# A fused attention and two-layer feed-forward kernel: the first stage issued in an order written out by hand

## The chip, the cores and the metric

The kernel runs on one core of one Trainium2 chip, as one launch. The metric is the time of the launch on the device in microseconds (us), lower being better: the median of three runs.

## What is computed

Attention with a narrow window plus pooled blocks, then a maxout layer, then a mish layer. All inputs and outputs are float32 except the six weight matrices, which are float64 and are handed over as pairs of 32-bit words. Shapes: q, k, v are 4 x 8 x 768 x 64; the tokens are 3072 with 512 features; the hidden widths are 768 and 2048.

```python
def _attn_ref(q, k, v):
    block, window = (32, 16)
    k_sum = k.reshape(B, H, nb, block, D).max(axis=3)
    v_sum = v.reshape(B, H, nb, block, D).mean(axis=3)
    scores_l = scale * np.matmul(q, k.transpose(0, 1, 3, 2))
    mask_l = np.abs(pos[:, None] - pos[None, :]) < window
    scores_s = scale * np.einsum('bhsd,bhnd->bhsn', q, k_sum) + np.log(block)
    scores_all = np.concatenate([np.where(mask_l, scores_l, -1e9), scores_s], axis=-1)
    a = softmax(scores_all)
    return np.matmul(a, np.concatenate([v, v_sum], axis=2))

def _moe_ref(x, w1, w2, w3, w_out):
    h = np.maximum(np.maximum(x @ w1, x @ w2), x @ w3)
    return h @ w_out

def _moe2_ref(x, w_in, w_out):
    h = x @ w_in
    return (h * np.tanh(softplus(h))) @ w_out
```

## The kernel before

**Tiles and blocks.** The 3072 tokens are 48 tiles of 64; two tiles make a unit `u` (24 units, six to a batch), and three units, 384 tokens, make one of eight blocks. A unit goes through attention in five steps (`step`, L528): scores and exps of the next unit (`s2`, L435), preparation of q and k (`q_prep`, `k_prep`), transposes of the probabilities (`s3`, L490; the tile is `ptp`, its copy `pT`), normalisation (`s2b`, L480), and the product with v (`s4`, L501; `xp`, split into `xh` and `xl`). A block goes through `gemm1` (L587; products `hp`, three for each of six row groups f, combined by maxima into `m`, split into `hh` and `hl`) and `gemm2` (L624; product `yp`, one for each of four column groups e, over all six f, written to DRAM as `x2d`). At the end a second layer runs over all tokens (`g3`, `mish_a` to `mish_c`, `g4`).

**Precision.** Each product is made of three matmuls on a high and a low part of each operand. The high and low parts of x and h come from a cast on ScalarE and a difference on VectorE.

**Weights.** Each slice of a float64 weight matrix (128 x 512 values, 512 KB) is a job with four parts: a fetch into one of three `words` buffers (`fetch`, L163, SyncE), the magnitude on ScalarE (`size_of`, L174, writes `wa`), five or six VectorE operations that turn the words into a float32 value and a rest (`narrow`, L180), and the split into high and low part (`done`, L229). For the first 14 jobs the low part is made by three matmuls (`wp`, L240 to L242) and a ScalarE cast (L243); for the others by a difference on VectorE (L237). The 24 jobs of the first layer fill slots `a`, `b` (w1 to w3, three jobs for each f) and `c` (w_out, one for each f); 32 more, for the second layer, follow from block 2 on and go to DRAM. `run_job` (L203) moves each job in flight on by one part.

**Keys and values of batch 0.** They are loaded whole (L763, L768). The first six tiles take their keys from these copies through GpSimd (`load_k`, L401). Later tiles read them from a transposed copy in DRAM: `store_far` (L370) writes it (`kTd`), `load_k` reads it back (L404). The block means of v are six pairs of matmuls into `vp` (L306), copied by L788 and L790. Batches 1 to 3 are prepared while the batch before runs; KLOAD0 and VLOAD0 (L525, L526) say at which unit of batch 0.

**What sets the order.** The program is written in one order (L761 on), and a scheduler that models the engines reorders the instructions of each engine before the kernel is built. On the chip each engine then executes its list in order and waits on semaphores. All DMAs are issued by SyncE, in its list's order; each issue also waits until an earlier DMA on the same one of eight semaphores has landed. The written order before: loads, six `k_prep`, unit 0 up to `s2b`, three jobs in between, the six means of v, then 16 attention steps with a job at every second one (`PER`, L802 to L806), then block after block: a job, a group of the products, and as many attention steps as are due (L846 to L852).

**Buffers.** PSUM has four banks for `hp`, `yp` and `wp` together (tag `g`) and four for attention. `m` and `y` share two buffers. `words` has three.

Of the kernel before, what the change touches and what calls it, by code (L numbers as in the profile page):

```python
# [3 lines left out]

# [6 lines left out]
F32 = mybir.dt.float32  # L11
# [8 lines left out]
P = 128  # L20
# [11 lines left out]
NEAR = 6  # L32
BT = 6
ITEMS = 5
PER = [1, 0]
AHEAD = 4
JOBN = 3
JOB0 = 2
# [15 lines left out]
def tile_kernel(ctx, tc, q, k, v, w1, w2, w3, w_out, w_in2, w_out2, out):  # L54
# [87 lines left out]

    last = {"early": True}

# [53 lines left out]
        nc.vector.tensor_tensor(out=a, in0=w, in1=a, op=ALU.add)  # L198
        return a, None

    fetched, sized, narrowed = [], [], []

    def run_job(after=None):  # L203

        if narrowed:
            w, rest, done = narrowed.pop(0)
            done(w, rest)
        if jobs:
            src, done, parts = jobs.pop(0)
            fetched.append((fetch(src), done, parts))  # L210
        if sized:
            words, a, done, parts = sized.pop(0)
            narrowed.append((*narrow(words, a, parts), done))
        if fetched and (len(fetched) > 1 or not jobs):
            words, done, parts = fetched.pop(0)
            with tc.issue_after(after) if after else nullcontext():
                a = size_of(words)
            sized.append((words, a, done, parts))

    def busy():  # L220
        return bool(jobs or fetched or sized or narrowed)

    jobs = []
    fslice = lambda f: slice(f * P, (f + 1) * P)
# [3 lines left out]
    def into(tag, place, key):  # L228
        def done(w, rest):  # L229
            if tag not in slot_of:  # L230
                slot_of[tag] = wslot(tag)
            t = slot_of[tag]
            wa[key] = t, 2 * place
            h, l = t[:, 2 * place], t[:, 2 * place + 1]
            nc.scalar.copy(h, w)
            if rest is None:
                nc.vector.tensor_tensor(out=l, in0=w, in1=h.bitcast(F32), op=ALU.subtract)  # L237
                return
            sums = gps.tile([P, 512], F32, name="wp", tag="g")
            nc.tensor.matmul(sums, lhsT=ident, rhs=w, start=True, stop=False)  # L240
            nc.tensor.matmul(sums, lhsT=one_r, rhs=rest, start=False, stop=False)
# [17 lines left out]
    def keep(f, i):  # L259
        def done(w, _):  # L260
            h = stage.tile([P, 512], F32R, name="wr", tag="wr", bufs=AB)
            nc.scalar.copy(h, w)
            nc.vector.tensor_tensor(out=w, in0=w, in1=h.bitcast(F32), op=ALU.subtract)
            nc.sync.dma_start(out=w2d[f][:, 2 * i], in_=h.bitcast(F32))
            last["store"] = nc.sync.dma_start(out=w2d[f][:, 2 * i + 1], in_=w)

        return done

# [163 lines left out]
    att_t = {}  # L432
    heads = lambda s: s.rearrange("q (r p) x -> q r p x", r=2)

    def s2(u):  # L435

        t = u % NG
        kind = "first" if t == 0 else "last" if t == NG - 1 else "mid"
        mask = masks[kind]
        sc = [bank("sc") for r in range(2)]  # L440
        add = u >= PEMASK
        if not add:
            for r in range(2):
                for j, m in enumerate(split_masks[kind]):
                    nc.tensor.matmul(
                        sc[r][:, :, 0:KX], lhsT=one_r, rhs=m.unsqueeze(1).to_broadcast([P, NP, KX]),
                        start=(j == 0), stop=False,
                    )
        for p in range(NP):
            for e in reversed(range(GT)):  # L450
                for r in range(2):
                    d = slice(r * D, (r + 1) * D)
                    c = slice(e * QT, (e + 1) * QT)
                    nc.tensor.matmul(
                        sc[r][c, p, 0:KX], lhsT=qT[u % RQ][d, p, c], rhs=kT[(GT * u + e) % RK][d, p],
                        start=add, stop=add or p == NP - 1,
                    )
        s = ap2.tile([P, H, KX], F32, name="s", tag="s", bufs=SB)
        src = [x[:, :, 0:KX] for x in sc]
        if add:  # L460
            for r in range(2):
                wide = mask.unsqueeze(1).to_broadcast([P, NP, KX])
                nc.vector.tensor_tensor(out=heads(s)[:, r], in0=src[r], in1=wide, op=ALU.add)
            src = [heads(s)[:, r] for r in range(2)]
        nm = ap2.tile([P, 2, NP], F32, name="nm", tag="nm")
        if add:
            nc.vector.tensor_reduce(out=nm, in_=heads(s), axis=AX.X, op=ALU.max, negate=True)  # L467
        else:
            for r in range(2):
                nc.vector.tensor_reduce(out=nm[:, r], in_=src[r], axis=AX.X, op=ALU.max, negate=True)  # L470
        sm = ap2.tile([P, H], F32, name="esum", tag="esum")
        for h in range(H):
            r, p = divmod(h, NP)
            nc.scalar.activation(  # L474
                out=s[:, h], in_=src[r][:, p], func=AF.Exp, bias=nm[:, r, p : p + 1], accum_out=sm[:, h : h + 1]
            )
        rs = ap2.tile([P, H, 1], F32, name="rs", tag="rs")
        att_t[u] = (s, sm, rs)

    def s2b(u):  # L480
        s, sm, rs = att_t.pop(u)
# [40 lines left out]

    KLOAD = {0: [0, 1], 1: [2, 3], 2: [4, 5]}
    VLOAD = {0: [0], 1: [1], 2: [2], 3: [3, 4, 5], 4: [6, 7]}
    KLOAD0 = {1: [0, 1], 2: [2, 3], 3: [4, 5]}  # L525
    VLOAD0 = {1: [0], 2: [1], 3: [2], 4: [3, 4, 5]}  # L526

    def step(u):  # L528

# [2 lines left out]
        more = b + 1 < B  # L532

        def first():
            if u == 1:
                store_far()
            for T in (GT * (u + 1), GT * (u + 1) + 1):
                if ok(u + 1):
                    load_v(T)
            if ok(u + 1):  # L540
                s2(u + 1)

        def second():
            if ok(u + 2):
                q_prep(*divmod(u + 2, NG))
            for g in more and kload.get(t - 1) or ():
                k_prep(b + 1, g)
            if ok(u + 3):
                load_nat("q", q, *divmod(u + 3, NG))
            for g in more and kload.get(t) or ():  # L550
                load_nat("k", k, b + 1, g)

# [6 lines left out]
        def fourth():  # L559
            for g in more and vload.get(t - 1) or ():  # L560
                if b:
                    make_vsum(b + 1, *VP[g])
                else:
                    v_prep(1, g)
            for g in more and vload.get(t) or ():
                if b:
                    load_vsum(b + 1, *VP[g])
                else:
                    load_nat("v", v, 1, g)
            s3(u, 1)  # L570

        def fifth():
            s4(u)
            for T in (GT * (u + 2), GT * (u + 2) + 1):
# [49 lines left out]
    def gemm2(i, e):  # L624
# [13 lines left out]
            nc.sync.dma_start(out=x2d[i][:, e, :], in_=y[:, :n])  # L638

        return [emit]  # L640


    N2 = 384
# [117 lines left out]
    for g in range(NG):  # L761
        nat["k", 0, g] = t = room[g].rearrange("p (h d) -> p h d", h=H)
        nc.sync.dma_start(out=t, in_=k[0, :, g * P : (g + 1) * P, :].rearrange("h p d -> p h d"))  # L763
        if g == 2:
            load_nat("q", q, 0, 0)
    run_job()
    for g in range(NG):
        nc.sync.dma_start(out=vroom[g], in_=v[0, :, g * P : (g + 1) * P, :].rearrange("h p d -> p h d"))  # L768
        if g == 2:
            run_job()  # L770
    load_nat("q", q, 0, 1)
    for g in range(NG):
        k_prep(0, g, kst[g])
    for T in range(RK):
        load_k(T)
    q_prep(0, 0)
    run_job()
    s2(0)
    load_v(0)
    load_v(1)  # L780
    s2b(0)
    q_prep(0, 1)
    run_job()
    load_nat("q", q, 0, 2)
    vp = aps.tile([P, H, D], F32, name="vp", tag="a")
    for g in range(NG):
        mean_v(vp[0:NB].rearrange("p h d -> p (h d)"), vroom[g], g * NS, NB, g == 0, g == NG - 1)
    nc.scalar.copy(vr[0][0:NB], vp[0:NB])  # L788
    for t in vr[1:]:
        nc.gpsimd.tensor_copy(t[0:NB], vr[0][0:NB])  # L790

    steps = [it for u in range(NU) for it in step(u)]
    nstep = nit = 0

    def attend(upto):
        nonlocal nstep
        while nstep < min(upto, len(steps)):
            steps[nstep]()
            nstep += 1

    IB = ITEMS * BT // GT
    while nstep < IB + 1:  # L802
        attend(nstep + 1)
        for _ in range(PER[nit % len(PER)]):
            run_job()
        nit += 1  # L806

    later = [(f, (lambda f=f: wslot(slots[f])) if f < 2 * NF1 else (lambda f=f: extra[f - 2 * NF1]))
             for f in range(NF1, NF2)]
# [23 lines left out]
        if s >= LAG:  # L833
            g4(seq[s - LAG])

    last["early"] = False
    second_open = False
    early = 0
    for i in range(NBLK):
        groups = []  # L840
        for f in range(NF1):
            groups += [(f, g) for g in gemm1(i, f)]
# [55 lines left out]
```

## Time and profile before

| | |
|---|---|
| median of three runs | 1119.39 us (1117.86 to 1119.8) |
| the profiled execution | 1121.29 us |
| its span, first to last instruction | 1119.5 us |
| mean granted TensorE clock | 0.991 |
| ScalarE, GpSimd busy | 548.6 us, 77.4 us |
| DMA | 125.49 MB in 179730 packets, mean 112 GB/s |
| first matmul of `gemm1` | 71.74 us |
| first matmul of block 1 | 157.25 us |

The profile is of one execution. Rows of instructions give the line, the engine, the tile written and the tiles read (buffer numbers left out), a count, and times; "idle before" is how long the engine had waited and what it waited for. PE is TensorE, DVE VectorE, ACT ScalarE, POOL GpSimd, SP SyncE.

### The profile page before, as it was taken

To read this page: it belongs to the slowest core of one execution; us is meant where nothing else is said; L and a number is where in the kernel's file an instruction comes from. 1 tells how busy PE (TensorE), PEld (TensorE's weight loads), DVE (VectorE), ACT (ScalarE), POOL (GpSimd) and SP (SyncE) were. 2 spreads that over 40 slices of the span, in tenths; PEclk is the share of its full clock that TensorE was granted. 3 is DMA by queue.
4 is the path that set the end of the run, shared out by engine and by line. 5 is a ranking of instruction groups with operands and counts; after the bars stand their busy time and mean duration, and the time that the engine had idled before them with its cause. 6 is when DMAs were issued, how large, how long until landed. Compare 5 with 4: busy or idle time off the path is not lost.

```text
span 1119.5 us, 18658 instructions
## 1 busy us (share of the span) xinstructions
PE 1087.2 (97%) x7004; PEld 986.9 (88%) x7004; DVE 816.1 (73%) x1623; ACT 548.6 (49%) x1336; POOL 77.4 (7%) x132
## 2 busy tenths in 40 slices
PE   6789989999999999999999999999999999999998
PEld 3468879999999899999999999989899998999987
DVE  5788953377887898942247887887878778787775
ACT  4676543345544555532135554545545454554543
POOL 3000021211114100100000000000000000000000
PEclk8989999999999999999999999999999999999999
DMA  9898772467888877412646010101001010000000
GB/s 239 199 248 230 170 193 63 136 155 197 247 224 253 200 228 190 152 37 71 233 178 248 20 37 1 57 1 29 29 1 58 1 44 14 15 29 1 29 1 29
DMA packets 179730, 125.49 MB, mean 112 GB/s; under 512 B 125048, under 2 KB 161400, under 8 KB 177592
## 3 DMA queue, kind: packets, MB, share of 16 engines
q1 hardware_dynamic: 179640, 124.30, 39.9%
q8 instruction: 55, 0.90, 0.3%
q14 instruction: 35, 0.29, 0.1%
HBM read 88.05 MB, written 35.05 MB: 110 GB/s over the span
## 4 chain that ended last, share of the span: by engine, by line
PE 75%; DVE 11%; ACT 6%; DMA 4%; issue 2%; SPq 1%; POOL 1%; ACTq 0%; POOLq 0%; DVEq 0%
PE up L692 8%; PE up L690 8%; PE acc L745 8%; PE up L691 8%; PE acc L746 8%; PE acc L747 8%; PE hp L599 5%; PE hp L600 5%; PE hp L601 5%; ACT s L474 3%; PE yp L633 2%; PE yp L634 2%; PE yp L635 2%; DMA kT<-kTd 1%; DVE words L190 1%
## 5 line engine op out<-in xcount | busy, mean ns | idle before, releaser
L708 ACT ACTIVATE r<-n,two 128x384 f32<-128x384 f32 x128 | 78.9, 616 | 155.3 <-DVE n L705 155.3
L599 PE MATMUL hp<-xh,a 128*128 128x384 f32 x384 | 133.6, 348 | 2.0 <-ACT y L637 2.0
L600 PE MATMUL hp<-xl,a 128*128 128x384 f32 x384 | 129.5, 337 | 0.0
L601 PE MATMUL hp<-xh,a 128*128 128x384 f32 x384 | 129.3, 337 | 0.0
L731 DVE TENSOR_TENSOR gl<-g,gh 128x384 fp32r<-128x384 f32 x128 | 71.4, 557 | 64.7 <-ACT gh L730 64.1
L701 ACT ACTIVATE e<-up 128x384 f32<-128x384 f32 x128 | 62.9, 492 | 97.3 <-PE up L692 96.6
L474 ACT ACTIVATE s<-s,nm 128x120 f32<-128x120 f32 x168 | 64.0, 383 | 45.1 <-DVE nm L467 45.1
L599 PEld LDWEIGHTS hp<-xh,a 128*128 128x128 f32 x384 | 72.7, 189 | 4.7 <-ACT y L637 2.4
L718 DVE TENSOR_TENSOR p<-up,r 128x384 f32<-128x384 f32 x128 | 70.5, 551 | 6.2 <-ACT r L709 6.2
L600 PEld LDWEIGHTS hp<-xl,a 128*128 128x128 f32 x384 | 72.7, 189 | 0.8 <-issue 0.5
L601 PEld LDWEIGHTS hp<-xh,a 128*128 128x128 f32 x384 | 72.7, 189 | 0.0
L723 DVE SCALAR_TENSOR_TENSOR g<-u,n 128x384 f32<-128x384 f32 x128 | 70.8, 553 | 0.9
L703 DVE TENSOR_SCALAR ep<-e 128x384 f32<-128x384 f32 x128 | 45.9, 358 | 34.8 <-ACT e L701 34.3
L721 DVE SCALAR_TENSOR_TENSOR u<-u,p 128x384 f32<-128x384 f32 x128 | 70.6, 552 | 0.4
L705 DVE SCALAR_TENSOR_TENSOR n<-e,ep 128x384 f32<-128x384 f32 x128 | 70.7, 552 | 0.3
L720 DVE SCALAR_TENSOR_TENSOR u<-n,r 128x384 f32<-128x384 f32 x128 | 70.2, 548 | 0.0
L730 ACT CAST gh<-g 128x384 fp32r<-128x384 f32 x128 | 64.2, 502 | 9.7 <-DVE g L723 9.7
L633 PE MATMUL yp<-hh,c 128*128 128x384 f32 x192 | 65.4, 346 | 3.5 <-ACT hh L618 1.9
L709 ACT ACTIVATE r<-r 128x384 f32<-128x384 f32 x128 | 67.1, 524 | 0.9
L599 PE MATMUL hp<-xh,b 128*128 128x384 f32 x192 | 67.4, 351 | 0.0
L611 DVE TENSOR_TENSOR m<-hp,m 128x384 f32<-128x384 f32 x48 | 26.5, 553 | 53.4 <-PE hp L601 48.7
L692 PE MATMUL up<-x2h,a 128*128 128x384 f32 x192 | 64.6, 337 | 0.0
(171 smaller groups left out, 2920.3 us busy)
## 6 DMA issues: line engine op xcount, KB each, us to landing
words<-in_moe_w_out SPq DMA_DIRECT2D x22, 512.0 KB, 4.5
words<-in_moe_w SPq DMA_DIRECT2D x18, 512.0 KB, 5.2
words<-in_moe_w_in SPq DMA_DIRECT2D x16, 512.0 KB
w2d<-wr SPq DMA_DIRECT2D x32, 256.0 KB, 2.7
w2d<-wa SPq DMA_DIRECT2D x32, 256.0 KB, 4.1
kT<-kTd SPq DMA_DIRECT2D x35, 192.0 KB, 5.1
vr<-in_v SPq DMA_DIRECT2D x35, 192.0 KB, 5.2
nat<-in_q SPq DMA_DIRECT2D x24, 256.0 KB, 4.5
```

The source lines that it names most:

```text
L474: nc.scalar.activation(out=s[:, h], in_=src[r][:, p], func=AF.Exp, bias=nm[:, r, p : p + 1], accum_out=sm[:, h : h + 1])
L599: nc.tensor.matmul(pt[:, :n], lhsT=wh, rhs=xh[:, c, :n], start=(c == 0), stop=False)
L600: nc.tensor.matmul(pt[:, :n], lhsT=wh, rhs=xl[:, c, :n], start=False, stop=False)
L601: nc.tensor.matmul(pt[:, :n], lhsT=wl, rhs=xh[:, c, :n], start=False, stop=(c == KC - 1))
L633: nc.tensor.matmul(pt[:, :n], lhsT=wh, rhs=hh[:, :n], start=(f == 0), stop=False)
L690: nc.tensor.matmul(pt[:, :N2], lhsT=wh, rhs=xh[:, c], start=(c == 0), stop=False)
L691: nc.tensor.matmul(pt[:, :N2], lhsT=wh, rhs=xl[:, c], start=False, stop=False)
L692: nc.tensor.matmul(pt[:, :N2], lhsT=wl, rhs=xh[:, c], start=False, stop=(c == KC - 1))
L708: nc.scalar.activation(out=r, in_=d["n"], func=AF.Ln, bias=two[:, 0:1])
L745: nc.tensor.matmul(o, lhsT=gh[:, c], rhs=w[:, 2], start=(f == 0), stop=False)
L746: nc.tensor.matmul(o, lhsT=gh[:, c], rhs=w[:, 3], start=False, stop=False)
L747: nc.tensor.matmul(o, lhsT=gl[:, c], rhs=w[:, 2], start=False, stop=(f == NF2 - 1))
```

## The change

The part of the program up to the first group of block 0 is written out call by call, and each engine is bound to the written order in it (`in_order`). To allow that, `run_job` is split into `fetch_next`, `size_next`, `narrow_next`, `round_next` and `close_next`, and `s2` into `scores`, `largest` and `exps`. The rest of block 0 is left to the scheduler, with one job ahead of each group; there the second product is written slice by slice (f by f, all four column groups side by side, `gemm2_slices`) instead of column group by column group. The loads of batch 1 move on by one unit (KLOAD0, VLOAD0), `store_far` moves from the first step of unit 1 to the second, and the block means of v go to a bank with tag `g`. The number of instructions of each kind is the same.

```diff
+    @contextmanager
+    def in_order():
+        traced = nc.cur_bb.bb.instructions
+        n = len(traced)
+        yield
+        latest = {}
+        for i in traced[n:]:
+            if i.engine in latest:
+                tc.add_manual_dep(
+                    i, latest[i.engine].name,
+                    mybir.DependencyInfo(mybir.DependencyClass.NoSync, mybir.DependencyReason.DATA),
...
+            latest[i.engine] = i
...
     def run_job(after=None):
+        old = bool(narrowed)
+        if old:
+            round_next()
+        fresh = bool(fetched)
+        fetch_next()
         if sized:
+            narrow_next()
+        late = old and rounded[0][1]
+        if old and not late:
+            close_next()
+        if fresh:
             with tc.issue_after(after) if after else nullcontext():
+                size_next()
+        if late:
+            close_next()
...
-            nc.scalar.copy(l, sums)
+            return lambda: nc.scalar.copy(l, sums)
...
-    KLOAD0 = {1: [0, 1], 2: [2, 3], 3: [4, 5]}
-    VLOAD0 = {1: [0], 2: [1], 3: [2], 4: [3, 4, 5]}
+    KLOAD0 = {2: [0, 1], 3: [2, 3], 4: [4, 5]}
+    VLOAD0 = {2: [0], 3: [1], 4: [2], 5: [3, 4, 5]}
...
+    def gemm2_slices(i):
...
+        def part(f):
+            if f == 0:
+                pts.extend(gps.tile([P, 512], F32, name="yp", tag="g") for e in range(KC))
...
+            for e, pt in enumerate(pts):
...
+                if f == NF1 - 1:
+                    y = g2.tile([P, MAXT * QT], F32, name="y", tag="my", bufs=2)
+                    nc.scalar.copy(y[:, :n], pt[:, :n])
+                    nc.sync.dma_start(out=x2d[i][:, e, :], in_=y[:, :n])
...
-    while nstep < IB + 1:
-        attend(nstep + 1)
-        for _ in range(PER[nit % len(PER)]):
+    with in_order():
...
+        q_prep(0, 0)
+        size_next()
+        scores(0)
+        narrow_next()
+        largest(0)
+        round_next()
+        exps(0, 0)
+        exps(0, 1)
...
+        v_mean(0)
+        v_mean(1)
+        q_prep(0, 1)
+        close_next()
+        v_mean(2)
+        scores(1)
+        s2b(0)
+        loads(0)
+        load_nat("q", q, 0, 2)
+        fetch_next()
+        s3(0, 0)
+        s3(0, 1)
+        v_mean(3)
+        largest(1)
+        size_next()
+        exps(1, 0)
+        v_mean(4)
+        narrow_next()
...
+        s4(2)
+        scores(3)
+        first_groups = [g for f in range(NF1) for g in gemm1(0, f)] + gemm2_slices(0)
+        first_groups.pop(0)()
+        narrow_next()
+        largest(3)
+        close_next()
+        exps(3, 0)
+        exps(3, 1)
+        first_groups.pop(0)()
+        fetch_next()
+        loads(3)
+        size_next()
...
+    G = len(first_groups) + 3
+    n_ = 3
+    while first_groups:
+        if busy():
             run_job()
+        first_groups.pop(0)()
+        n_ += 1
+        attend(IB + (IB * n_) // G + (AHEAD * min(n_, 8)) // 8)
+    attend(2 * IB + AHEAD)
```

Three places of the resulting lists follow; line numbers of the kernel after differ from those before. The first is TensorE behind unit 0's scores (`sc`), where the means of v (`vp`), q's transposes (`tp`) and a job's three matmuls (`wp`) meet. Before:

```order
L240 MATMUL wp<-words,ident 128x512
L352 MATMUL tp<-ident,nat 128x128 x4
L306 MATMUL vp<-vroom_207,mean 24x512 x4
L306 MATMUL vp<-vroom_208,mean 24x512 x2
L445 MATMUL sc<-both_mid,one_r 128x4x120 x4
L241 MATMUL wp<-wr,one_r 128x512
L242 MATMUL wp<-a_350,neg_r 128x512
```

After:

```order
L346 MATMUL vp<-vroom_207,mean 24x512 x2
L392 MATMUL tp<-ident,nat 128x128 x4
L346 MATMUL vp<-vroom_207,mean 24x512
L484 MATMUL sc<-both_mid,one_r 128x4x120 x4
```

The means no longer stand between the parts of one job; three of the six are taken ahead of unit 1's scores and the others later.

The second is SyncE from the sixth weight slice on, up to the first keys read back from DRAM (`kT<-kTd`). Before:

```order
L167 DMA words<-in_moe_w 128x4x256 x2
L376 DMA kTd_174<-room_206 512x1x16
L376 DMA kTd_174<-room_206 512x1x128 x3
L303 DMA nat<-in_q 128x8x64
L303 DMA nat<-in_k 128x8x64 x2
L167 DMA words<-in_moe_w 128x4x256
L404 DMA kT_194<-kTd_174 128x4x96
L415 DMA vr_197<-vroom_207 80x512
L415 DMA vr_196<-vroom_207 16x512
L415 DMA vr_196<-vroom_207 80x512
L415 DMA vr_197<-vroom_207 16x512
L404 DMA kT_195<-kTd_174 128x4x96
```

After:

```order
L182 DMA words<-in_moe_w 128x4x256
L455 DMA vr_196<-vroom_207 16x512
L455 DMA vr_196<-vroom_207 80x512
L455 DMA vr_197<-vroom_207 80x512
L455 DMA vr_197<-vroom_207 16x512
L416 DMA kTd_174<-room_206 512x1x16
L416 DMA kTd_174<-room_206 512x1x128 x3
L343 DMA nat<-in_q 128x8x64
L444 DMA kT_194<-kTd_174 128x4x96
L444 DMA kT_195<-kTd_174 128x4x96
L182 DMA words<-in_moe_w 128x4x256
```

The v rows of unit 2 (`vr`) moved ahead of the stores, the k loads of batch 1 behind the reads, and the seventh weight slice, which stood ahead of the stores, behind them.

The third is ScalarE around the last slice of w_out (`c`) and the copies of block 0's second product (`y`). Before:

```order
L235 CAST c_1458<-wa 128x512
L380 ACTIVATE qT_191<-tp 128x512
L363 COPY kst<-tp 128x512
L474 ACTIVATE s,esum<-s,nm 128x120 x8
L637 COPY y<-yp 128x384 x2
L496 COPY pT<-ptp 120x512 x2
```

After:

```order
L272 CAST c_1679<-wa 128x512
L420 ACTIVATE qT_190<-tp 128x512
L549 COPY pT<-ptp 120x512
L521 ACTIVATE s,esum<-s,nm 128x120
L718 COPY y<-yp 128x384
L521 ACTIVATE s,esum<-s,nm 128x120
L718 COPY y<-yp 128x384
L521 ACTIVATE s,esum<-s,nm 128x120 x6
```

The first `y` copy stood behind eight exps of a unit; it now stands behind one.

More of the change, by code (lines that the diff above doesn't have):

```diff
@@ L199, in narrow, with fetch_next @@
         return a, None
[L201 to L207, printed above, removed]
+    fetched, sized, narrowed, rounded = [], [], [], []
+    def fetch_next():
         if jobs:
@@ L262, in done, with close @@
             nc.scalar.copy(h, w)
-            nc.vector.tensor_tensor(out=w, in0=w, in1=h.bitcast(F32), op=ALU.subtract)
-            nc.sync.dma_start(out=w2d[f][:, 2 * i], in_=h.bitcast(F32))
-            last["store"] = nc.sync.dma_start(out=w2d[f][:, 2 * i + 1], in_=w)
+            def close():
+                nc.vector.tensor_tensor(out=w, in0=w, in1=h.bitcast(F32), op=ALU.subtract)
+                nc.sync.dma_start(out=w2d[f][:, 2 * i], in_=h.bitcast(F32))
+                last["store"] = nc.sync.dma_start(out=w2d[f][:, 2 * i + 1], in_=w)
+            return close
         return done
@@ L433, in tile_kernel, with scores @@
     heads = lambda s: s.rearrange("q (r p) x -> q r p x", r=2)
-    def s2(u):
+    def scores(u):
         t = u % NG
         kind = "first" if t == 0 else "last" if t == NG - 1 else "mid"
-        mask = masks[kind]
         sc = [bank("sc") for r in range(2)]
@@ L457, in s2, with largest @@
                     )
+        att_t[u] = [x[:, :, 0:KX] for x in sc], add, masks[kind]
+    def largest(u):
+        src, add, mask = att_t[u]
         s = ap2.tile([P, H, KX], F32, name="s", tag="s", bufs=SB)
-        src = [x[:, :, 0:KX] for x in sc]
         if add:
@@ L471, in s2, with exps @@
         sm = ap2.tile([P, H], F32, name="esum", tag="esum")
-        for h in range(H):
-            r, p = divmod(h, NP)
+        rs = ap2.tile([P, H, 1], F32, name="rs", tag="rs")
+        att_t[u] = s, src, nm, sm, rs
+    def exps(u, r):
+        s, src, nm, sm, rs = att_t[u]
+        for p in range(NP):
+            h = r * NP + p
             nc.scalar.activation(
@@ L476, in s2 @@
             )
-        rs = ap2.tile([P, H, 1], F32, name="rs", tag="rs")
-        att_t[u] = (s, sm, rs)
+        if r:
+            att_t[u] = s, sm, rs
+    def s2(u):
+        scores(u)
+        largest(u)
+        exps(u, 0)
+        exps(u, 1)
     def s2b(u):
@@ L545, in second @@
                 q_prep(*divmod(u + 2, NG))
-            for g in more and kload.get(t - 1) or ():
+            for g in more and not (b == 0 and t == NG - 1) and kload.get(t - 1) or ():
                 k_prep(b + 1, g)
@@ L569, in fourth @@
                     load_nat("v", v, 1, g)
+            if u == NG - 1:
+                for g in VLOAD0[t]:
+                    v_prep(1, g)
             s3(u, 1)
@@ L573, in fifth @@
             s4(u)
+            if b == 0 and t == NG - 2:
+                for g in KLOAD0[t]:
+                    k_prep(1, g)
             for T in (GT * (u + 2), GT * (u + 2) + 1):
@@ L760, in tile_kernel @@
     vroom = [r[:, j].rearrange("p (h d) -> p h d", h=H) for r in vroom for j in range(4)]
[L761 to L790, printed above, removed]
     steps = [it for u in range(NU) for it in step(u)]
-    nstep = nit = 0
+    nstep = 0
     def attend(upto):
@@ L834, in second_step @@
             g4(seq[s - LAG])
-    last["early"] = False
     second_open = False
     early = 0
-    for i in range(NBLK):
+    for i in range(1, NBLK):
         groups = []
```

116 lines of the change are left out of this document (102 added, 14 removed).

## The prediction

> **What bounds the kernel now.** I read the page first, then busy time by stretches, then the chain of work and the timelines of the first 160 us. The page gives engine time over the span, and the same in 40 slices of 28 us.
>
> ```profile
> PE 1087.2 (97%) x7004; PEld 986.9 (88%) x7004; DVE 816.1 (73%) x1623; ACT 548.6 (49%) x1336; POOL 77.4 (7%) x132
> PE   6789989999999999999999999999999999999998
> ```
>
> TensorE is busy 97% of the span; nearly all the slices under 9 tenths lie ahead of about 170 us. So there is little to win, and it lies there. Busy time in stretches there (start:end, length, then PE, PEld, DVE, ACT, POOL, granted clock, DMA share, GB/s):
>
> ```profile
> 0.00:60.00 60.00, 43.09 (x322) 25.70 (x322) 37.89 (x70) 33.82 (x93) 12.68 (x54) 0.94 0.89 225
> 72.00:94.00 22.00, 22.00 (x139) 17.76 (x138) 17.90 (x36) 15.44 (x40) 0.00 (x0) 1.00 1.05 242
> 94.00:141.00 47.00, 46.63 (x397) 41.17 (x395) 46.18 (x87) 29.05 (x83) 3.51 (x5) 1.00 0.82 191
> 141.00:152.50 11.50, 9.71 (x101) 8.04 (x102) 10.24 (x16) 5.52 (x14) 3.65 (x4) 1.00 0.67 167
> 157.25:161.30 4.05, 4.05 (x15) 4.05 (x16) 0.72 (x2) 2.80 (x6) 3.14 (x4) 0.59 0.77 236
> 0.00:152.50 152.50, 130.45 (x1033) 97.42 (x1034) 122.11 (x227) 93.99 (x256) 19.83 (x63) 0.96 0.90 214
> ```
>
> From 72 us TensorE is covered; from 94 to 141 VectorE is full as well (46.18 of 47). VectorE does 122.11 us of work in the first 152.5 us, so it idles 30.4 us, 22.1 of them before 60. That is the term to follow: 24 weight slices must pass through VectorE before block 0's second product can close. The chain of waits shows how block 0 ends:
>
> ```profile
> 151.94 0.60 DVE c L237
> 152.54 1.07 DVE nm L467
> 153.70 3.13 ACT s L474 x16
> 156.83 0.37 ACT y L637
> 157.25 0.44 PE hp L599
> ```
>
> VectorE closes the last slice of w_out at 152.5; TensorE starts block 1 at 157.25. It sits 4.7 us behind that close, because ScalarE runs a unit's exps between them. From 157.25 the first 15 matmuls run at a mean clock of 0.59.
>
> **The change, part by part.** The instructions are the same in number; only their order changes, and with it which queues up behind which. I ask two things: when VectorE finishes the first `hl` (row group f = 0 of block 0), and how much VectorE work then remains to the last close.
>
> *Hand-written stage.* The six tile means, twelve matmuls in a row, are now spread out:
>
> ```profile
> 25.56 6.68 PE L306 MATMUL vp<-vroom,mean 128*24 128x512 f32 x12
> 32.00:34.00 2.00, 2.00 (x19) 1.34 (x22) 0.42 (x1) 1.32 (x3) 1.09 (x2) 1.00 0.04 9
> ```
>
> Behind that run stood the product that frees a weight buffer, so the DMA engines stood empty from 32 us (a share of 0.04 up to 34). That hole shrinks, but it does not vanish: weight 5 now waits for job 2, which sits behind unit 1's maxima. What gates the new stage is unit 3, the first whose keys come back through DRAM:
>
> ```profile
> 38.52 3.71 SPq L376 DMA_DIRECT2D kTd<-room  x4
> 43.21 2.48 SPq L303 DMA_DIRECT2D nat<-in_k  x2
> 48.31 2.56 SPq L415 DMA_DIRECT2D vr<-vroom  x4
> 50.97 1.26 SPq L404 DMA_DIRECT2D kT<-kTd  x2
> 54.68 1.05 PE L454 MATMUL sc<-kT,qT 64*64 64x120 f32 x32 [0.19 <-DMA kT<-kTd]
> kTd<-room SPq DMA_DIRECT2D x3, 256.0 KB, 5.3
> ```
>
> The stores leave at about the same time as before: what is ahead of them on SyncE is weight 6, which waits for job 3, and by my count of the chain that job ends near 34 to 36. What goes from between is the four `vr` loads (2.56) and the two k loads (2.48): 54.68 - 5.0 = 49.7. But the stores, issued until 42.2, need 5.3 to land, then a load's issue and 3.65 to arrive (50.97 to 54.68): 42.2 + 5.3 + 0.8 + 3.65 = 52. I take 51. TensorE has nothing else in its fixed order, so it waits there, and all of the first group stands behind that wait. After it come the scores (1.0), 36 matmuls, and the closing max, cast and difference (1.7). A matmul's step is read here:
>
> ```profile
> 110.10 1.15 PE L508 MATMUL xp<-pT,vr 120*64 120x64 f32 x32
> 111.18 1.05 PE L454 MATMUL sc<-kT,qT 64*64 64x120 f32 x32
> 113.69 0.34 PE L601 MATMUL hp<-xh,b 128*128 128x384 f32 x1
> 113.86 0.60 PE L352 MATMUL tp<-ident,nat 128*128 128x128 f32 x4
> 114.21 0.42 PE L599 MATMUL hp<-xh,a 128*128 128x384 f32 x1
> ```
>
> Starts are 0.17 us apart (113.69 to 113.86), so 36 take 6.3, and a group of four transposes 0.35: 51 + 1.0 + 6.6 + 1.7 = 60.3. After a pause the clock has fallen before:
>
> ```profile
> 60.00:62.00 2.00, 0.00 (x0) 0.00 (x0) 1.56 (x4) 2.00 (x10) 0.00 (x0) 1.00 1.29 168
> 64.00:66.00 2.00, 1.02 (x3) 0.38 (x3) 2.00 (x4) 2.00 (x5) 0.00 (x0) 0.50 1.02 229
> ```
>
> An idle 2 us at 60 was followed by 0.50 at 64; at that clock a matmul steps by twice 0.17. If 18 of the 36 run so, that is 3 us, and if none does, nothing; I take 1.2, since a pause need not fall so that the clock drops: first `hl` at 61.5, between 58 and 65.
>
> [...]
>
> *VectorE's work up to that `hl`.* In the new order there stand ahead of it five narrowings, seven first steps of one, six key maxima, four normalisations and the scores' maxima. Their forms, up to 152.5 us:
>
> ```profile
> L190 DVE SCALAR_TENSOR_TENSOR words<-words,wa 128x512 uint32<-128x512 uint32 x24 | 16.5, 689 | 0.4
> L187 DVE TENSOR_SCALAR wa<-wa 128x512 uint32<-128x512 uint32 x24 | 11.9, 495 | 0.4
> L185 DVE TENSOR_SCALAR wa<-wa 128x512 f32<-128x512 f32 x24 | 10.9, 454 | 8.2 <-ACT wa L177 8.2
> L193 DVE TENSOR_SCALAR wa<-words 128x512 uint32<-128x512 uint32 x24 | 10.1, 423 | 0.3
> L195 DVE SCALAR_TENSOR_TENSOR wr<-words,wa 128x512 fp32r<-128x512 uint32 x14 | 10.0, 713 | 2.6 <-PE wp L241 2.0 <-DVE wa L187 0.2
> L366 DVE TENSOR_REDUCE ksum<-tp 128x16 f32<-128x512 f32 x12 | 8.1, 684 | 3.0 <-ACT room L363 2.9
> L485 DVE TENSOR_TENSOR s<-s,rs 128x960 f32<-128x960 f32 x6 | 6.9, 1157 | 0.2
> L467 DVE TENSOR_REDUCE nm<-s 128x8 f32<-128x960 f32 x6 | 6.9, 1144 | 0.0
> L463 DVE TENSOR_TENSOR s<-sc,mask_mid 128x480 f32<-128x480 f32 x8 | 4.9, 648 | 0.0
> L518 DVE TENSOR_TENSOR xl<-xp,xh 128x512 fp32r<-128x512 f32 x7 | 4.8, 684 | 0.5 <-ACT xh L517 0.5
> L470 DVE TENSOR_REDUCE nm<-sc 128x4 f32<-128x480 f32 x6 | 3.7, 648 | 0.0
> ```
>
> 5 x 0.689 + 6 x 0.495 + 7 x 0.454 + 5 x 0.423 + 5 x 0.713 + 6 x 0.684 + 4 x 1.157 + 1.144 + 2 x 0.648 + 3 x 0.684 + 6 x 0.648 = 32.4. Small ones (the split masks, sums, reciprocals, three of the group itself) make about 4.4 by my estimate: 36.8. Forms overlap: all of them up to 152.5 add up to 134 against 122.11 of busy time, so 36.8 x 0.91 = 33.6.
>
> *What then remains.* Ahead of the last close the new order also has two more key maxima, one more masked unit with its maxima, sums and `xl`: about 4.2 x 0.91 = 3.8. Remaining: 122.1 + 3.8 - 33.6 = 92.3. Idle beside it: from 94 to 141 VectorE idled 2% (0.82 of 47), from 72 to 152.5 7.7% (4.10 + 0.82 + 1.26 of 80.5), so 1.6 to 7.1; I take 3.0, nearer the low end, because most of the new stretch is that dense interleaving. Close: 61.5 + 92.3 + 3.0 = 156.8, 4.3 later than now.
>
> *The end of block 0.* In the new order the exps ahead of the first `y` copy are a single one, of the unit whose maxima follow the close: mask half 0.65, maxima 1.14, one exp and the copy, about 2.8 us, against 4.75. Block 1 starts at 159.6. By then TensorE has done more than now: 12 transposes (3 x 0.35), 8 of `ptp` (0.7), one unit of `sc` and of `xp` (1.05 + 1.08, the latter from 110.10 to 111.18), 3.9 in all. Counted off: 155.7 against 157.25, a gain of 1.6. The half clock at 157.25 cost 12 steps of 0.15, 1.8; a shorter pause probably spares most of it: 1.4. Sum: 3.0 us gained.
>
> *Edits that cost nothing by themselves.* The product slice by slice: the scheduler had already taken the last slices of the four column groups side by side. Splitting jobs into smaller calls changes only the order. The later k and v loads of batch 1 are hidden as long as their users from unit 6 on stand behind block 0; if that cover goes, it is one landing, about 5 us. The added fixed order binds no queue at run time that was not in order anyway; behind a waiting SyncE issue stand all later loads, though, and that is the third rival.
>
> The profiled execution spans 1119.5 and took 1121.29; the median of the runs is 1119.39, so span and median can be set equal. From 160 us TensorE is covered, so a gain there moves the end: 1119.4 - 3.0 = 1116.4.
>
> **Rivals.** *Dense loop.* VectorE never waits after 60 us and the clock stays up: `hl` at 59, close at 152.9, and the half clock wholly spared: 7 us gained, 1112; with the stage another 3 earlier 1109. For it: 46.18 of 47. Against it: the DMA engines were at 1.05 from 72 to 94.
>
> *A wash.* The stage ends earlier on TensorE but VectorE reaches the same work no sooner: at 60 us it had done 37.89 before, against about 33 now. Then 4 to 6 us of idle in the loop give the gain back: 1117.5 to 1121.
>
> *Weights arrive late (slower).* Weights are now fetched just in time with three buffers, and more k, q and v loads stand between them on SyncE. A fetch needs this long:
>
> ```profile
> DMA to landing us min/median/max: 4.5/4.8/5.6
> ```
>
> After the first seven, 17 fetches are each issued only when a job has freed a buffer. If each costs VectorE 0.7 us of waiting, idle is 12 and not 3: 1125.4. It decides from about 0.36 us per fetch (6 us). For it: by my estimate from the sizes in the new order, fetches 8 to 24 and the loads between them are 17.7 MB in about 72 us, 246 GB/s, and the best long stretch above has 242. Against it: part of that may slip behind block 0. [...]
>
> **How the numbers follow.** Forecast (a gain of 2.3 to 6) 0.32, dense loop 0.18, wash 0.22, late weights 0.28. Faster: 0.32 + 0.18 = 0.50; same 0.22; slower 0.28. About 0.2% (2.2 us) is what a measurement here can tell from no change. As both signs hold much of the chance: the forecast's own range is 1113 to 1117. For 8 in 10 I leave out the far ends: 1108 (the stage 3 us earlier and no idle) to 1126 (late weights).
>
> **What would show it.** First `hp` near 52 rather than 71.7 and first `hl` near 61.5; scores of unit 3 waiting for `kT<-kTd` near 51; the last `c` difference near 157; block 1's first matmul 3 us or less behind it, at full clock. I am wrong if VectorE waits on `wa` or `words` in the loop for more than 6 us, if the first `hl` lies outside 58 to 65, or if the shift at block 1 is not the shift at the end.

## The result, and the profile after

The changed kernel takes 1132.84 us (median of four runs, 1131.43 to 1133.94), the kernel before 1119.6 in the runs beside it: a ratio of 1.0106, 95% interval 1.0084 to 1.0128. It is 13.2 us slower. The forecast was 1116.4, its range 1108 to 1126. The profiled execution took 1133.94 with a span of 1132.2, against a span of 1119.5 before.

The page of the kernel after: engine time over the span, TensorE in 40 slices.

```profile
PE 1095.0 (97%) x7004; PEld 991.6 (88%) x7004; DVE 818.5 (72%) x1623; ACT 547.9 (48%) x1336; POOL 79.5 (7%) x132
PE   7799789999999899999999999999999999999998
```

The instruction counts are the same. Of the slices (28 us each) five ahead of the last are under 9 tenths, where there were four; the 14th, at about 370 us, is new and lies far behind block 0. The early slices come first. TensorE's timeline of the kernel after (start, duration, line, tile, and what ended the idle time ahead): the places that the prediction named.

```profile
50.91 1.05 PE L493 MATMUL sc<-kT,qT 64*64 64x120 f32 x32 [1.08 <-DMA kT<-kTd]
51.89 0.45 PE L658 MATMUL hp<-xh,a 128*128 128x384 f32 x1
...
172.35 0.45 PE L658 MATMUL hp<-xh,a 128*128 128x384 f32 x1 [0.33 <-ACT y L718]
172.64 0.34 PE L659 MATMUL hp<-xl,a 128*128 128x384 f32 x1
```

And VectorE's:

```profile
62.42 0.55 DVE L678 TENSOR_TENSOR hl<-m,hh 128x384 fp32r<-128x384 f32 x1
...
168.51 0.68 DVE L274 TENSOR_TENSOR c<-wa,c 128x512 fp32r<-128x512 f32 x1
```

The first product starts at 51.9 instead of 71.7, the first `hl` stands at 62.4, and then something goes wrong: the last slice of w_out closes at 169.2 instead of 152.5, and block 1 starts at 172.35 instead of 157.25. VectorE between that `hl` and that close, in the kernel after (stretch, length, PE, PEld, DVE, ACT, POOL):

```profile
62.97:169.19 106.22, 94.10 (x715) 73.82 (x708) 90.15 (x169) 63.52 (x169) 10.31 (x12) 0.90 0.83 203
```

It had 90.15 us to do, and stood idle 16.1. What ended its idle time there, and ScalarE's from 72 to 170 us (line, tile, releaser: us in total, times, longest):

```profile
DVE wa L200 <- ACT wa L192: 9.6, 8, 3.0
DVE esum L535 <- ACT s L521: 3.4, 2, 1.9
```

```profile
ACT wa L192 <- DMA words<-in_moe_w: 6.4, 5, 2.4
ACT wa L192 <- DMA words<-in_moe_w_out: 6.1, 1, 6.1
```

VectorE waits for the absolute values (`wa`, 9.6 of its 16.1 us), ScalarE makes them and waits for `words`: weights. The prediction's own sign of being wrong, more than 6 us of such waits, is there. The longest wait of ScalarE, 6.1 us, can be read in the chain that ended last:

```profile
137.79 6.14 DMA nat<-in_v
144.14 1.06 POOL nat L376
145.27 0.73 POOL nat L376
146.08 0.66 POOL vs L378
146.76 0.39 SPq L343
147.26 4.43 DMA words<-in_moe_w_out
151.78 0.67 ACT wa L192
152.47 0.43 DVE wa L200
```

A load of v lands, GpSimd adds it up and frees its buffer, SyncE's next load had stood there for that buffer, and the weight fetch stood behind that load.

That is not all of the loss. From block 2 on the two kernels differ only in the order of a job's parts, yet block 2 starts at 227.51 against 218.62 (8.9 late) and the span ends 12.7 late. Blocks 2 to 5, those in which the second layer's weights are prepared, took 256.6 us against 252.9.

### The profile page after: what moved, and what is told of

The parts are those of the page before. It is cut to its first block, busy times and chain, and to the rows that moved or that the text cites. A ratio compares the mean times of both kernels' runs of the same rounds, so it can differ in the third digit from the quotient of the medians.

```text
span 1132.2 us, 18670 instructions
## 1 busy us (share of the span) xinstructions
PE 1095.0 (97%) x7004; PEld 991.6 (88%) x7004; DVE 818.5 (72%) x1623; ACT 547.9 (48%) x1336; POOL 79.5 (7%) x132
## 4 chain that ended last, share of the span: by engine, by line
PE 72%; DVE 10%; DMA 7%; ACT 7%; issue 2%; POOL 1%; SPq 0%; ACTq 0%; POOLq 0%; DVEq 0%
PE up L773 8%; PE up L771 8%; PE acc L826 8%; PE up L772 8%; PE acc L827 8%; PE acc L828 8%; PE hp L658 5%; PE hp L660 5%; PE hp L659 5%; ACT s L521 3%; PE yp L692 2%; PE yp L693 2%; PE yp L694 2%; DMA w2d<-wa 2%; DMA kTd<-kst 1%
## 5 line engine op out<-in xcount | busy, mean ns | idle before, releaser
L658 PE MATMUL hp<-xh,b 128*128 128x384 f32 x192 | 68.0, 354 | 1.0 <-ACT y L718 0.6
L660 PE MATMUL hp<-xh,b 128*128 128x384 f32 x192 | 64.8, 337 | 1.0 <-ACT b L279 1.0
## 6 DMA issues: line engine op xcount, KB each, us to landing
w2d<-wr SPq DMA_DIRECT2D x32, 256.0 KB, 4.8
w2d<-wa SPq DMA_DIRECT2D x32, 256.0 KB, 5.4
nat<-in_q SPq DMA_DIRECT2D x24, 256.0 KB, 3.9
```

Source lines behind the costliest of these rows:

```text
L658: nc.tensor.matmul(pt[:, :n], lhsT=wh, rhs=xh[:, c, :n], start=(c == 0), stop=False)
L660: nc.tensor.matmul(pt[:, :n], lhsT=wl, rhs=xh[:, c, :n], start=False, stop=(c == KC - 1))
```

## The experiments

The theory that follows from this: weights come late in block 0's loop, and VectorE starves. The table gathers what decides, from the profiles: starts of blocks 1 and 2, the time of blocks 2 to 5, and VectorE's idle time from 62.97 us to its last `c` close. The times are medians of the kernel's own runs; the kernel before, run again beside each group of them, had medians of 1118.7 to 1119.9. Below, the figures in brackets behind a time are its ratio to the kernel before and the 95% interval of that ratio.

| kernel | us | block 1 | block 2 | blocks 2–5 | idle |
|---|---|---|---|---|---|
| before | 1119.6 | 157.3 | 218.6 | 252.9 | 7.8 |
| after | 1132.8 | 172.4 | 227.5 | 256.6 | 16.1 |
| no_fetch | 1124.3 | 157.9 | 214.5 | 260.2 | 2.9 |
| more_words | 1126.1 | 156.2 | 216.8 | 259.3 | 7.2 |
| pool_fetch | 1133.3 | 168.3 | 223.7 | 259.9 | 11.6 |
| loose | 1126.1 | 165.6 | 220.6 | 257.8 | 14.0 |
| late_old | 1124.7 | 170.6 | 226.7 | 250.9 | 13.7 |
| more_late | 1118.5 | 155.2 | 216.0 | 252.8 | 7.3 |
| loose_more_late | 1115.0 | 149.8 | 211.1 | 252.1 | 3.2 |
| before_late_new | 1125.0 | 154.4 | 215.8 | 259.0 | 6.0 |
| late_fetch_first | 1130.1 | 168.1 | 222.8 | 258.2 | 11.1 |
| wa_free | 1127.9 | 166.6 | 221.2 | 254.4 | 12.6 |
| dve_free | 1131.4 | 166.7 | 222.9 | 258.2 | 11.6 |
| whole | 1129.2 | 158.0 | 219.0 | 260.2 | 8.1 |
| whole_late | 1123.4 | 159.0 | 220.1 | 253.7 | 8.1 |
| drain | 1131.2 | 166.6 | 221.4 | 256.0 | 12.4 |
| best_drain | 1114.2 | 149.5 | 210.8 | 252.5 | 3.8 |
| best_whole | 1114.2 | 152.3 | 213.5 | 252.8 | 5.4 |

Mind the spread first: after, late_old, late_fetch_first, wa_free and drain execute the same instructions in the same order up to block 2, and start it at 227.5, 226.7, 222.8, 221.2 and 221.4. A start of a block in one profile is good to about 3 us either way, no better.

**Weights not fetched (no_fetch).** The weights of jobs 8 to 24 are left out.

```diff
+        if n < 24:
...
+            words = held[n % 3]
+            if n >= 7:
+                return words
```

> The changed kernel without the transfers of the weights of jobs 8 to 24: their words are read from the three buffers that were filled first, so the weights of most of block 0 and of the later blocks are other ones; instructions on the engines are the same. Theory (weights arrive late in the loop of block 0, and VectorE stands idle some 12 us for it): VectorE's waits for wa, 9.6 us in the changed kernel, fall under 3, block 1's first hp comes at 158 to 162 instead of 172.35, and the time is 1119 to 1124. Rival (the hand-made order, or the slices of the second product with four banks held, costs the time, and the late weights only fill a wait that is there anyway): block 1 still starts after 168, time over 1129.

Measured 1124.33 (1.0046, 1.0031 to 1.0061), 0.3 us above the expected range. Idle fell to 2.9:

```profile
62.97:153.16 90.19, 83.77 (x686) 65.94 (x679) 87.27 (x165) 62.99 (x169) 10.04 (x11) 1.00 0.61 138
```

So the fetches are what VectorE waits for, by coming late or by the traffic that they add (138 GB/s here against 203): this run takes away both. Block 2 started at 214.5, earlier than in the kernel before. But about 5 us stay above before, and all of that, and more, is in blocks 2 to 5 (260.2): the second loss.

**More buffers (more_words).**

```diff
+        if 5 <= n < 17 and n % 5 > 2:
+            words = spare[n % 5 - 3]
...
-        if jobs:
+        n = last.get("n", -1) + 1
+        if jobs and len(fetched) <= (3 if n < 17 else 1):
...
+        fetch_next()
+        fetch_next()
         loads(3)
```

> The changed kernel with two more buffers for words (the two halves of the room that the keys of batch 0 have left by then) for jobs 6 to 17, and the 9th and 10th fetch issued before the loop begins, so that two more jobs are under way in the first half of the loop; from job 18 on three buffers again. Theory (a job's three buffers, each held from the issue of the fetch to the end of the narrowing, limit the weights to one in 5.1 us): waits of VectorE for wa fall from 9.6 to under 5, block 1 starts at 160 to 167, time 1121 to 1128. Rival (the queue of SyncE or the order of the engines is the limit, not the buffers): block 1 after 170, time 1131 to 1135.

Measured 1126.1 (1.0064, 1.0049 to 1.0079). Block 1 starts even earlier than expected, at 156.2, and idle is 7.2:

```profile
62.97:154.12 91.15, 83.76 (x652) 66.84 (x652) 83.91 (x159) 57.93 (x147) 7.66 (x9) 0.94 0.91 217
```

Two more buffers and two fetches more under way, changed together, undo block 0's loss, with all 24 fetches made.

**Another queue (pool_fetch).**

```diff
-            last["words"] = nc.sync.dma_start(out=o, in_=x)
+            n = last["n"] = last.get("n", -1) + 1
+            last["words"] = (nc.gpsimd if 7 <= n < 24 else nc.sync).dma_start(out=o, in_=x)
```

> The changed kernel with the fetches of words of jobs 8 to 24 issued by GpSimd instead of SyncE, so that they no longer stand behind SyncE's loads of keys, queries and values; still three buffers. Theory in its first form (buffers limit): some of the wait goes, above all the 6.1 us for the fetch issued at 147.26 behind a load of values; 1126 to 1133. Rival (the place in SyncE's queue is the whole cause): 1119 to 1125. Rival (neither: bound order or slices): 1131 to 1136.

Measured 1133.3 (1.0125, 1.0107 to 1.0143): no gain. What GpSimd's fetches waited for, then TensorE, and what is left of the waits for weights on VectorE and ScalarE:

```profile
POOL words L183 <- PE wp L279: 21.9, 4, 8.8
POOL words L183 <- DVE wa L214: 21.2, 6, 4.7
```

```profile
PE ptp L548 <- POOL s L539: 4.3, 1, 4.3
```

```profile
DVE wa L201 <- ACT wa L193: 0.6, 2, 0.3
ACT wa L193 <- DMA words<-in_moe_w_out: 0.9, 1, 0.9
ACT wa L193 <- DMA words<-in_moe_w: 0.9, 2, 0.6
```

The last readers of a `words` buffer (`wp` on TensorE, the sum at L214 on VectorE) still hold the fetches back. But the waits for weights have nearly gone: on VectorE from 9.6 us to 0.6, on ScalarE from 12.5 to 1.8. VectorE's idle time stays at 11.6, about that of the four repeats of the changed block 0 (11.1 to 13.7), now in other waits: 4.4 us for copies of k and 3.9 for exps on ScalarE. And GpSimd, which stands at the fetches in order, makes TensorE wait 4.3 us for a unit it normalises. So another queue alone gains no time; that the place behind SyncE's loads is harmless is not shown, since new waits came with the edit. The trace speaks against it: 8.91 MB of fetches went over a queue of their own, and ScalarE's waits for them fell to 1.8 us. Whether the queue or the changed moments of issue did that is not shown.

**Order not bound (loose).**

```diff
-    with in_order():
+    with nullcontext():
```

> The changed kernel with the hand-written sequence in the same program order, but not bound engine by engine: the scheduler may move instructions. Theory (late weights in the loop; the bound order is not the cause): within 4 us of the changed kernel, 1129 to 1137. Rival (the binding costs: some engine stands behind an instruction that the scheduler would have put later): 1119 to 1126.

Measured 1126.11 (1.0064, 1.0043 to 1.0085): 0.1 us above the rival's range and 2.9 below the theory's, so the rival was right here. The binding costs. VectorE had narrowed seven jobs by 62 us, five in the bound order (in all five profiles of it), eight in the kernel before.

**The old order of a job in the later blocks (late_old), both mends (more_late), and the converse (before_late_new).**

```diff
+        if after:
+            if narrowed:
+                round_next()
+                close_next()
+            fresh = bool(fetched)
+            fetch_next()
+            if sized:
+                narrow_next()
...
+            return
```

> The changed kernel with the job's order of the kernel before for the weights of the second layer alone (blocks 2 to 5: rounding, closing with its two stores, fetch, narrowing, size), the new order in block 0 kept. Theory of two losses (the late weights in block 0's loop, and the new order of a job in the later blocks, where closing behind the narrowing holds a wa buffer longer: blocks 3 to 5 took 195.2 us instead of 190.5): these three blocks take 189 to 192 us, time 1126 to 1130. Rival (one loss: blocks 3 to 5 are longer since block 0's end shifts the attention against them): they stay at 195 to 198 and the time at 1131 to 1135.

> Both mends together: two more buffers for words in the loop of block 0 and the old order of a job in blocks 2 to 5. Theory of two losses: they add, block 1 starts at 155 to 160, blocks 3 to 5 take 189 to 192, time 1118 to 1122, equal to the kernel before within 3 us. Rival (one loss, given back later by whichever of the two is not mended): 1124 to 1127.

> The kernel before with one part of the change alone: for the weights of the second layer a job closes behind the next job's narrowing. Theory of two losses: blocks 3 to 5 take 194 to 198 us instead of 190.5, time 1122 to 1126. Rival (the job's order costs nothing): 1118 to 1121.

Measured 1124.71 (1.0051, 1.0031 to 1.0071), 1118.46 (0.9991, 0.9978 to 1.0003) and 1125.03 (1.0050, 1.0027 to 1.0073). All three speak for two losses that add, though late_old came out 1.3 us below its range: mending the later blocks alone gains 8 us, mending both brings back the time before, and the new order alone put into the kernel before makes it 5 us slower. Seven profiles with the old order have blocks 2 to 5 at 250.9 to 253.7, nine with the new (without late_fetch_first and wa_free, which change it) at 256.0 to 260.2; they do not overlap, and their means differ by 6.1. TensorE feels it. The stretch of blocks 2 to 5 (start:end, length, PE, PEld, DVE, ACT, POOL, granted clock, DMA share, GB/s) in after and in late_old:

```profile
227.51:484.14 256.63, 250.45 (x2091) 237.93 (x2090) 206.75 (x368) 127.82 (x372) 39.50 (x42) 1.00 0.69 196
226.72:477.57 250.85, 248.83 (x2092) 238.24 (x2089) 207.49 (x370) 128.64 (x372) 40.11 (x42) 1.00 0.74 202
```

TensorE stands idle 6.2 us in the first and 2.0 in the second.

SyncE shows what moved. Before, one job (start, time to issue):

```profile
355.55 0.34 SPq L264 DMA_DIRECT2D w2d<-wr  x1
356.27 0.34 SPq L265 DMA_DIRECT2D w2d<-wa  x1
356.67 0.51 SPq L167 DMA_DIRECT2D words<-in_moe_w_in  x1
```

After:

```profile
366.31 0.39 SPq L182 DMA_DIRECT2D words<-in_moe_w_in  x1
366.96 0.33 SPq L302 DMA_DIRECT2D w2d<-wr  x1
367.69 0.33 SPq L303 DMA_DIRECT2D w2d<-wa  x1
```

The fetch now stands ahead of the job's two stores, and it waits for VectorE to free a `words` buffer. SyncE's waits from 280 to 480 us in the kernel after:

```profile
SPq L182 <- DVE wa L213: 34.9, 15, 4.7
SPq L182 <- DVE wa L200: 26.7, 4, 10.8
```

The stores behind that wait hold `wa`, one of two, until they land, and the next sizing waits on ScalarE for it. ScalarE's wait from 210 to 480 us, before:

```profile
ACT wa L177 <- DMA w2d<-wa: 0.9, 1, 0.9
```

and after:

```profile
ACT wa L192 <- DMA w2d<-wa: 5.8, 7, 2.0
```

It is 1.0 in late_old, 6.6 in before_late_new and 7.0 in late_fetch_first, the next run: it comes and goes with the order.

**Which of the two moves it is (late_fetch_first), and whether it is `wa` (wa_free).** The first leaves the closing where it was and keeps only the fetch ahead; the second lets the store read another tile, so that the low parts of those weights are left out.

```diff
...
+                round_next()
+            fresh = bool(fetched)
+            fetch_next()
+            if old:
+                close_next()
...
```

```diff
-                last["store"] = nc.sync.dma_start(out=w2d[f][:, 2 * i + 1], in_=w)
+                last["store"] = nc.sync.dma_start(out=w2d[f][:, 2 * i + 1], in_=h.bitcast(F32))
```

> The changed kernel with, for the weights of the second layer, a job's order of rounding, fetch, closing with its two stores, narrowing, sizing: as in the changed kernel the fetch is written ahead of the stores, as in the kernel before the closing is ahead of the narrowing. If the closing behind the narrowing is what costs in blocks 3 to 5: they take 189 to 192 us and the time is 1122 to 1127. If the fetch ahead of the stores is: 194 to 198 and 1130 to 1134.

> The changed kernel with the second store of every job of the second layer reading the rounded tile (wr) instead of the remainder (wa): the low parts of those weights become copies of the high parts, the traffic and the instructions stay. The buffer of wa is then free when VectorE has subtracted, not when the store has landed. Theory (a job's wa, one of two, is held to the landing of its store, which the new order issues later, so the next sizing on ScalarE and the narrowing on VectorE behind it wait: 5.8 us of ScalarE's waits in blocks 2 to 5 for that store): ScalarE's wait for the store goes, blocks 3 to 5 take 189 to 193 us, time 1124 to 1129. Rival (it is VectorE's order itself, the subtraction behind five operations of the next job): 194 to 198 us and 1130 to 1134.

The first measured 1130.12 (1.0087, 1.0068 to 1.0106) with blocks 2 to 5 at 258.2: the fetch ahead of the stores is the cause, not VectorE's order. The second measured 1127.88 (1.0077, 1.0048 to 1.0106) with 254.4, between the groups: ScalarE's wait for the store is gone, and it recovers about two thirds of the 6.1 (258.6, the mean of the nine, less 254.4). By this one profile the buffer of `wa` is the larger part of the way from the late store to the loss; the rest stays open.

**VectorE alone not bound (dve_free).**

```diff
+            if i.engine == nc.vector.engine:
+                continue
```

> The changed kernel with all engines but VectorE bound to the written order. Not bound at all it was 6.7 us faster, and VectorE had narrowed seven jobs by 62 us instead of five. If VectorE's binding is what keeps it idle there: six or seven jobs narrowed by 62 us, time 1125 to 1129. If the binding of the others is (ScalarE's sizing, SyncE's fetches): five jobs, 1130 to 1135.

Measured 1131.39 (1.0102, 1.0083 to 1.0121), five jobs by 62 us: VectorE's own binding is not what costs. Which of the others' does was not taken apart.

**Both mends, not bound (loose_more_late).** The edits above together.

> Both mends, and the hand-written sequence not bound engine by engine. Theory of a third loss in the binding: another 2 to 5 us gained, 1114 to 1119. Theory without it (the scheduler's freedom gained 6.7 us only since it fetched a little earlier, which the two buffers now do): 1118 to 1122.

Measured 1114.97 (0.9954, 0.9939 to 0.9969), apart from more_late's interval: the binding is a third loss, about 3.5 us beside the other two. VectorE in the first 50 us, bound (more_late):

```profile
0.00:50.00 50.00, 36.46 (x296) 21.71 (x296) 27.38 (x50) 27.62 (x83) 14.10 (x54) 0.97 0.86 218
```

not bound (loose_more_late):

```profile
0.00:50.00 50.00, 37.30 (x316) 22.87 (x320) 31.35 (x61) 30.91 (x89) 13.72 (x54) 0.89 1.01 255
```

With 4 us more of VectorE's work done by 50 us, block 1 starts 5.4 earlier.

**The second product by columns (whole), and what that meant (whole_late, drain, best_drain, best_whole).** The first two have the columns of the kernel before, and whole_late the old order of a job in the later blocks as well; drain and best_drain keep the slices and write all jobs ahead of them. The two called best are loose_more_late with the one or the other.

```diff
-        first_groups = [...] + gemm2_slices(0)
+        first_groups = [...] + [g for e in range(KC) for g in gemm2(0, e)]
...
+        while len(first_groups) == KC and busy():
+            run_job()
```

```diff
+        while len(first_groups) == NF1 and busy():
+            run_job()
```

> The changed kernel with block 0's second product as in the kernel before, column by column with all six slices each, so that all 24 jobs are run before its first matmul; the rest of the change stays. Reckoning: four columns of 18 matmuls of 0.17 to 0.18 us behind the last closing are 12.5 us, where the changed kernel has one slice of 2.1 and a last copy; so if the slices do what they are there for, block 1 starts 8 to 11 us later, near 182, and the time is 1139 to 1144. Rival (the four banks held through the second product cost as much as the slices save): 1130 to 1135.

> The product by columns with all jobs before it, and the old order of a job in the later blocks; hand-bound first stage and three buffers stay. Sum: 1129.2 as measured with the columns, less 6 to 8 for the later blocks: 1121 to 1124. If the columns' gain is only given back later, 1124 to 1127.

> The changed kernel with its slices, but with all jobs that are left written down behind the last group of the first product, before the first slice and before the attention that is spread over the slices. With the product by columns, which needs the same, block 1 began at 157.98 and block 2 at 219.01, where four executions with the changed kernel's block 0 had 166.6 to 172.4 and 221.2 to 227.5. If the place of the jobs against the attention did that: block 1 starts at 153 to 160, block 2 at 215 to 221, time 1124 to 1130. If the slices themselves cost (their banks, their turns in PE's order): block 1 after 165, block 2 at 222 to 228, time 1130 to 1134.

> All mends together: the sequence not bound, two more buffers for words, the old order of a job in the later blocks, and the jobs written before the slices. Without the last it was 1115.0. If the place of the jobs against the attention costs on its own: 1109 to 1114. If it only made up for late weights, which are mended already: 1113 to 1117.

> The same with the product by columns instead of slices. If slices save nothing once the jobs stand before them: within 2 us of its sister with slices. If they save the columns' matmuls behind the last closing: 5 to 10 us slower than it.

Measured 1129.19, 1123.42, 1131.21, 1114.18 and 1114.19.

drain and best_drain test nothing: the scheduler undid the edit. In their traces every engine executes the same operations in the same order as in the changed kernel and in loose_more_late. They are repeats (1131.21 beside 1132.84, 1114.18 beside 1114.97), and the place of the jobs stays untested.

whole missed on both sides: block 1 started 14 us earlier, not later. The reckoning put the whole second product behind the last closing, but written by columns it is executed between the closings too: its first matmul starts at 131.5, 21 us ahead of the last closing, and 18 of its 72 come behind that (5 in the changed kernel). Part of the early start is attention put off into block 1: from 62.97 us to the last closing VectorE did 81.4 us of work instead of 90.15. But block 2 starts earlier too (219.0, against 221.2 to 227.5), with 8.1 of idle, and why is open.

Where weights come in time, columns (best_whole) and slices (best_drain) take the same (0.9961, 0.9948 to 0.9975, and 0.9961, 0.9947 to 0.9975, both against before). So the slices save nothing here. That they cost something while weights are late is not shown: the intervals of whole (1.0064 to 1.0109) and the changed kernel (1.0084 to 1.0128) overlap, and so do those of whole_late (1.0023 to 1.0050) and late_old.

## Why the prediction was wrong

**The written stage: right in its times, in part by luck.** Unit 3's scores waited for `kT<-kTd` until 50.9 (forecast 51), the first `hp` came at 51.9 (52), and the first `hl` ended at 63.0 (61.5). Terms that were off made up for each other. The stores of k did not leave at about the same time as before (38.5), but 3.3 us later, since the four `vr` loads now stood ahead of them:

```profile
38.50 3.27 SPq L455 DMA_DIRECT2D vr<-vroom  x4
41.80 2.77 SPq L416 DMA_DIRECT2D kTd<-room  x4
46.21 1.26 SPq L444 DMA_DIRECT2D kT<-kTd  x2
```

The reads followed the last store by 1.6 us, where 5.3 for its landing and 0.8 had been reckoned. The clock, for which 1.2 us was set aside, did not fall behind the wait of 1.08 us for those keys (granted 1.00 from 50 to 64 us; it had fallen behind a wait of 3.38 us up to 43.7, granted 0.50 from 44 to 48), but the closing took 4.1 us instead of 1.7 (58.9 to 63.0), because VectorE waited 2.4 us for unit 3's exps ahead of it.

**What VectorE has to do: right.** Up to that `hl` 33.6 us were forecast (36.8 x 0.91 is 33.5), 35.9 measured; behind it 92.3 were forecast, 90.15 measured.

**"Idle beside it … I take 3.0": failed.** It was 16.1 in the profile, 11.1 to 13.7 in the four others with the same block 0. The 3.0 was read off the dense stretch of the kernel before, in which weights came early enough: eight jobs were narrowed by 62 us there, five here. The rival on late weights priced this at 12 us of idle and 1125.4. That is where late_old came out, 1124.7, with that loss alone. It named three buffers and the loads between the fetches on SyncE. With two more buffers and two more fetches under way the loss goes (more_words: idle 7.2, block 1 at 156.2); how much the loads on SyncE add stays open (pool_fetch). No fetches at all give 2.9 of idle, the figure I took.

**"Splitting jobs into smaller calls changes only the order": failed.** It stood among the edits that cost nothing. The order is what costs: the fetch ahead of the stores on SyncE, 6.1 us in blocks 2 to 5 by the profiles, 5 to 8 by the times of before_late_new and late_old. The prediction followed the order up to block 1 alone.

**"From 160 us TensorE is covered, so a gain there moves the end": failed for the same reason.** Jobs run on to block 5, and a stall of VectorE and ScalarE there reaches TensorE: 6.2 us of idle in blocks 2 to 5, 2.0 with the old order of a job (late_old).

**The tail: right.** From the last close to block 1's first matmul 3.2 us passed (169.2 to 172.35), forecast 2.8, and that start was at full clock (granted 1.00 from 172.35 to 176.4). The clock fell elsewhere, behind the late slice at 156 (granted 0.50 from 156.1 to 160.1):

```profile
156.09 0.69 PE L713 MATMUL yp<-hh,c 128*128 128x384 f32 x1 [2.70 <-ACT c L272]
156.57 0.52 PE L714 MATMUL yp<-hl,c 128*128 128x384 f32 x1
156.89 0.52 PE L713 MATMUL yp<-hh,c 128*128 128x384 f32 x1
```

**"The added fixed order binds no queue at run time that was not in order anyway": failed.** It was put at nothing, but the scheduler's order was better than the written one: 6.7 us on the changed kernel (loose; 5.1 against its repeat, drain), 3.5 with the other losses mended.

The sum closes. Block 2 starts at 223.9 on average over the five profiles with the changed block 0, at 217.2 over the two with the old one: 6.7. With 6.1 from the later blocks that is 12.8, where the times differ by 13.2.

## What to carry to other kernels

Starting an engine's work earlier moves its supply's due date too (here VectorE's idle time in the loop went from 7.8 to 16.1 us): count how many transfers are done at the new start, how many buffers turn, and how long one is held, before taking idle time from the old steady state. When a step is split into smaller calls, read every DMA queue to the last place where the step is used: a fetch that waited for a buffer ahead of the stores that free another one cost 6.1 us here in blocks 2 to 5. A change of the written order need not be one of the executed order: read the lists that ran, as drain and best_drain show. The mended kernel (two spare buffers, stores ahead of the fetch, no binding) takes 1114.2 to 1115.0, 0.4 to 0.5% under the kernel before.

## What I had not expected of the hardware

Five profiles with the same instructions in the same order up to block 2 reach it between 221.2 and 227.5 us, a spread of 6.3 us in one stage. The whole runs of each of these five kernels spread by 2.5 to 7.2 us. One profile's stage time could not have told the losses apart; groups of profiles that do not overlap could.
